# Combine rows and weights in one partition-first table; lists give its row and the token

## Chip, cores and metric

The kernel runs on one core of one Trainium2 chip. The metric is the device time of one execution in microseconds (us), the median of several runs. Engines: TensorE (PE; PEld is its weight load), VectorE (DVE), ScalarE (ACT), GpSimd (POOL) and SyncE (SP), which here only issues DMAs; a queue (SPq, ACTq, POOLq) is the sequencer that issues for its engine.

## What is computed

Three layers in a row, all in float32, on 4 x 768 = 3072 tokens of 512 numbers (8 heads of 64):

```python
# 1. retention, per head h, over t
state = gamma[h] * state + outer(k[t], v[t]);  y[t] = scale * q[t] @ state
# 2. soft mixture: 8 experts with 4 slots each
logits = x @ phi                              # [3072, 32]
slot_input = softmax(logits, axis=0).T @ x    # [32, 512]
slot_out[e] = relu(slot_input[e] @ w1[e]) @ w2[e]
x2 = softmax(logits, axis=1) @ slot_out       # rank 32: combine rows c @ slot_out
# 3. top-2 mixture of 8 experts on x2
noisy = x2 @ w_gate + log1p(exp(x2 @ w_noise)) * noise
top2, top2_w = two largest, softmax over the two
out[mask] += top2_w * (relu(x2[mask] @ v1[e]) @ v2[e])   # for each expert e
```

The weights of layer 3 are called v1 (512 x 1024) and v2 (1024 x 512) in the kernel.

## The kernel before

**Stages.** Retention runs over 24 chunks of 128 tokens (NCH = 24) until about 150 us. The soft mixture's slot experts follow; their weights W2 are loaded in eight DMAs of 2 MB, the last of them in two halves, and the stage accumulates in the PSUM tile `po` (L602). Within a chunk partition j holds token 2 * (j % 64) + j // 64.

**Low rank.** Since x2 is c @ slot_out with 32 columns in c, layer 3 never forms x2: for each expert, G[e] = slot_out @ v1[e] (32 x 1024) is made once (`g_dot`, split into two parts by `g_split`, copied to the four partition groups of the tile `gs` by 16 DMAs of `g_copy` on SyncE, L741, or by matmuls for expert 0, `g_rep`), and the hidden layer of a token is relu(c[token] @ G[e]).

**The table.** `ctab` in DRAM holds for each token 32 combine numbers and 8 routing weights, and a row N of zeros for unused list places. `combine()` (L561) makes the combine rows `cs` and writes them with two GpSimd DMAs (L577), one for each half of the partitions; `combine_t()` transposes them with six matmuls (L584) for the router's logits. The routing weights `wsl` are written later by two ScalarE DMAs (L692).

**Routing (193 to 225 us).** Logits (L633), noise and the two choices on VectorE (L642 to L663), ranks in the expert's list by matmuls (L669 to L674), rounding to a block `blk` and a place in the block `rr`. Between them stand `fill` matmuls on ones (L144), which compute nothing that is used; F1 to F4, FA and FT are their numbers. The weights go through ScalarE, GpSimd and VectorE (L682 to L690; L685 is a reciprocal).

**Lists.** `lists(e)` (L750) makes for experts 0 and 1 the list of tokens: a mask `bm` on VectorE, two products of it on GpSimd (`bt`, L757 and L758: with the chunk's base and with the token in the chunk), three one-hot tiles `oh` on VectorE, 24 matmuls into `pli`, and two VectorE instructions that add the two sums (L768, L770). `lists_all()` does this for experts 2 to 7 jointly, in steps between the blocks of experts 0 and 1: each step's tiles are first touched by a tiny ScalarE copy of a block's output (`mark`), so that they can't run before it. Its products with the choices, `sb` on GpSimd (L804), had no such mark.

**Experts (from 225 us).** For each expert, 6 blocks of 128 list places and one of 64: `fetch` gathers the table's rows by an indirect DMA on GpSimd (L851), `turn` splits and transposes them (L863 to L873), `hidden` multiplies with G and makes the ReLU in two parts (L904, L907 on ScalarE, L909 on VectorE), `main` multiplies with v2 in two parts (`split_hi` on ScalarE, L879; `split_lo` on VectorE, L885; matmuls L937 to L943), scales the output (`yo`, L946) and adds it to `out` by an indirect DMA (L918). Blocks run in the order 0, 1, 2, 3, 6, 4, 5 for expert 0. `load_paced` loads the next v2 in four DMAs of 512 KB, each behind a tiny ScalarE copy of a block's output (L957, DMA L958); v1 two experts further the same way. V1[2] is loaded in three quarters at L698 and a fourth at L995, behind a GpSimd copy (L994) of the first gathered row.

**Order.** A scheduler puts the instructions of each engine and queue in order: it takes what is ready by its own estimate of time, the earlier in the program first. `after(ins)` keeps what the block traces on the same engine behind `ins`. `HOOK[e, b, kf]` runs a function while block b of expert e is traced, at its kf-th slice.

## Time and profile before

| | us |
|---|---|
| median of 3 runs | 589.7 (586.41 to 592.46) |
| the profiled execution | 592.0 |
| its span, first to last instruction | 590.2 |
| TensorE busy in the span | 554.7 (94%) |
| VectorE, ScalarE, GpSimd busy | 255.3, 243.7, 222.5 |
| mean granted clock of TensorE | 0.964 of full |

Times in the profile are counted from the first instruction. A row of the timeline has its start, its duration, the engine, the line of the kernel, the operation, the tile written and the tiles read, shapes, how many instructions are merged in it, and in brackets how long the engine was idle before it and whose end let it go.

### The profile page before, as it was taken

How to read it: one execution, taken by the hardware profiler on the slowest of the kernel's cores; microseconds unless marked ns; L12 is line 12 of the kernel's file. 1: busy time of each engine (PE TensorE's matmuls, PEld its weight loads, DVE VectorE, ACT ScalarE, POOL GpSimd, SP SyncE). 2: the span in 40 equal slices, each digit the busy share in tenths (PEclk: the TensorE clock that was granted, in tenths of full speed). 3: DMA queues.
4: the chain of work that ended last, by engine and by line, in shares of the span. 5: the costliest groups of instructions: out<-in, count | busy, mean ns of one | idle time of the engine just before them, and what ended most of it. 6: DMA issues, size and time to landing. Idle time of an engine off the chain costs nothing. (4 is left out here: it accounts for less than half of the span.)

```text
span 590.2 us, 10723 instructions
## 1 busy us (share of the span) xinstructions
PE 554.7 (94%) x4196; PEld 421.8 (71%) x4196; DVE 255.3 (43%) x529; ACT 243.7 (41%) x543; POOL 222.5 (38%) x214
## 2 busy tenths in 40 slices
PE   7999999999899878979999999999999999999990
PEld 4787888787443436858787787787787787788880
DVE  3566777764202366456625235235235234334200
ACT  2555656553101235245246246246345335335210
POOL 3524534330103055642455444344344436332231
PEclk7899999999699789989999999999999999999997
DMA  9999999998799942465446646656656644553232
GB/s 218 286 270 306 299 328 281 308 405 364 291 404 389 367 124 67 102 179 151 108 98 182 125 132 186 124 151 168 137 140 170 143 112 65 132 105 46 37 43 31
DMA packets 79485, 111.76 MB, mean 189 GB/s; under 512 B 10066, under 2 KB 51602, under 8 KB 78530
## 3 DMA queue, kind: packets, MB, share of 16 engines
q1 hardware_dynamic: 65808, 95.96, 49.3%
q0 software_dynamic: 9696, 14.37, 16.7%
q10 hardware_dynamic: 3922, 0.66, 0.6%
q8 instruction: 35, 0.57, 0.4%
q14 instruction: 24, 0.20, 0.1%
HBM read 87.92 MB, written 20.41 MB: 184 GB/s over the span
## 5 line engine op out<-in xcount | busy, mean ns | idle before, releaser
L937 PE MATMUL pyc<-wh,hhl 128*128 128x512 f32 x384 | 154.6, 403 | 0.2 <-ACT hhl L907 0.2
L938 PE MATMUL pyc<-wl,hhl 128*128 128x512 f32 x384 | 152.1, 396 | 0.0
L939 PE MATMUL pyc<-wh,hhl 128*128 128x512 f32 x384 | 151.5, 395 | 0.0
L918 POOL DMA_INDIRECT out_dram<-yo,lsa x42 | 66.1, 1575 | 136.1 <-ACT w L957 31.6
L909 DVE SCALAR_TENSOR_TENSOR hhl<-phc,hhl 128x512 fp32r<-128x512 f32 (+1 forms) x128 | 66.9, 551 | 84.9 <-ACT hhl L907 84.5
L939 PEld LDWEIGHTS pyc<-wh,hhl 128*128 128x128 f32 x384 | 72.6, 189 | 16.6
L937 PEld LDWEIGHTS pyc<-wh,hhl 128*128 128x128 f32 x384 | 72.1, 188 | 16.1 <-ACT hhl L907 0.4
L946 ACT ACTIVATE yo<-pyc,cg 128x512 f32<-128x512 f32 x48 | 33.0, 688 | 121.0 <-PE pyc L939 108.1
L938 PEld LDWEIGHTS pyc<-wl,hhl 128*128 128x128 f32 x384 | 72.4, 189 | 14.6
L907 ACT ACTIVATE hhl<-phc 128x512 fp32r<-128x512 f32 (+1 forms) x128 | 59.5, 513 | 8.0 <-PE phc L904 6.6
L885 DVE TENSOR_TENSOR wl<-w,wh 128x1024 fp32r<-128x1024 f32 x32 | 39.1, 1225 | 49.6 <-ACT wh L879 49.6
L851 POOL DMA_INDIRECT cg<-ctab,lsa x42 | 43.8, 1042 | 15.2 <-issue 14.9
L879 ACT CAST wh<-w 128x1024 fp32r<-128x1024 f32 x32 | 33.4, 1047 | 32.3 <-DMA w<-in_moe_w_dram 24.7
L298 DVE TENSOR_TENSOR am<-pa,cta 128x512 f32<-128x512 f32 x48 | 33.1, 692 | 28.6 <-PE py L322 15.3
L918 POOL DMA_INDIRECT out_dram<-yo,ls x14 | 25.0, 1787 | 47.4 <-ACT w L957 16.2
L256 POOL TENSOR_TENSOR comp<-raws,cta 64x512 f32<-64x512 f32 x24 | 24.9, 1039 | 40.7 <-PE py L322 16.5
L276 DVE TENSOR_TENSOR qT<-pt,cta 64x512 f32<-64x512 f32 x48 | 33.0, 688 | 16.6 <-PE pt L271 16.2
L256 POOL TENSOR_TENSOR vl<-raws,cta 64x512 f32<-64x512 f32 x24 | 24.9, 1038 | 33.5 <-PE py L322 22.6
L904 PE MATMUL phc<-cts,gs 128*128 128x256 f32 (+1 forms) x192 | 36.5, 299 | 0.5 <-ACT cts L873 0.5
L904 PEld LDWEIGHTS phc<-cts,gs 128*128 128x128 f32 x192 | 29.8, 191 | 7.3 <-issue 2.5
L294 PE MATMUL pa<-qT,kT 64*128 64x128 f32 x384 | 31.7, 296 | 0.7 <-DVE qT L276 0.7
L294 PEld LDWEIGHTS pa<-qT,kT 64*128 64x128 f32 x384 | 27.0, 198 | 5.2 <-issue 3.7
(195 smaller groups left out, 701.6 us busy)
## 6 DMA issues: line engine op xcount, KB each, us to landing
w<-in_moe_w_dram SPq DMA_DIRECT2D x80, 512.0 KB, 5.1
w<-in_moe_w_dram SPq DMA_DIRECT2D x11, 2048.0 KB, 10.5
comp<-in_q_dram SPq DMA_DIRECT2D x12, 512.0 KB, 6.7
out_dram<-zt SPq DMA_DIRECT2D x6, 1024.0 KB, 9.8
raws<-in_k_dram SPq DMA_DIRECT2D x11, 512.0 KB, 5.6
raws<-in_v_dram SPq DMA_DIRECT2D x11, 512.0 KB, 7.8
gs<-gr SPq DMA_DIRECT2D x112, 32.0 KB, 2.3
w<-in_moe_w_dram SPq DMA_DIRECT2D x2, 1024.0 KB, 21.1
```

The lines of the kernel that those rows point to most:

```text
L256: pool_ins[0] = nc.gpsimd.tensor_tensor(VL[j][rs], RAW[u][1][gs, :, r, :], gv[gs, r, t, :, None].to_broadcast([64, H, D]), op=OP.mult)
L294: mm = nc.tensor.matmul(pa[s][:, hp, :], KT[j][r, hp, :], QT[t][r, hp, g, :], start=True, stop=True)
L851: nc.gpsimd.indirect_dma_start(out=cg[:rows(b), i, :], out_offset=None, in_=ctab, in_offset=index(e, b, rows(b)))
L879: ins = nc.scalar.copy(wh, V2[e][:, 1024 * i:1024 * i + 1024])
L885: nc.vector.tensor_tensor(wl, V2[e][:, 1024 * i:1024 * i + 1024], WH[e][i], op=OP.subtract)
L904: nc.tensor.matmul(ph[:, w * i:w * i + w], GS[e][:, kf + i], CT[e, g][:, :w], start=True, stop=True)
L907: relu.append(nc.scalar.activation(h[:, :, :w], pv, AF.Relu))
L909: last = nc.vector.scalar_tensor_tensor(h[:, :, w + t0:w + t0 + 2 * P], pv[:, :, :2 * P], 0.0, h[:, :, :2 * P], op0=OP.max, op1=OP.subtract)
L918: nc.gpsimd.indirect_dma_start(out=out, out_offset=index(e, b, n), in_=y, in_offset=None, bounds_check=N - 1, oob_is_err=False, compute_op ...
L937: nc.tensor.matmul(py, hhl[:, kf, ts], wh, start=(kf == 0), stop=False)
L938: nc.tensor.matmul(py, hhl[:, kf, ts], wl, start=False, stop=False)
L939: nc.tensor.matmul(py, hhl[:, kf, tl], wh, start=False, stop=(kf == KF - 1))
```

## The change

- `ctab` has N rows in the order partition first: row = 24 * partition + chunk. The zero row and its DMA are gone.
- Combine rows and weights lie in one tile `row` (128 partitions x 24 chunks x 40 numbers); `cs` and `wsl` are views of it. One ScalarE DMA writes it when the weights are there, in place of two GpSimd DMAs and two ScalarE DMAs.
- `combine_t` has 24 matmuls against the identity, with 32 columns of weights each, in place of 6 transposes, since four chunks are no longer neighbours.
- Lists: the second factor is the partition (`row`) in place of the token in the chunk (`tok`). From the two sums `places` makes two tables, `lg` (row of the table, for gathers) in two instructions and `ls` (token, for adding to `out`) in three more behind it.
- Fills in the routing: 14 before g_dot(0) and 6 behind it, in place of 26 before it. The reciprocal of the weights stands behind the sum of the two choices.
- All four quarters of V1[2] are loaded behind the table's DMA; the copy L994 and the DMA L995 are gone.
- `sb` of the joint lists gets a mark. The copy of G for expert 2 to `gs` moves from slice 6 of block 0 to slice 5 of block 3 of expert 0; its split stays.
- The path for lists that overflow uses both tables (not shown; it isn't taken with these inputs).

```diff
--- before.py
+++ after.py
@@ -41,7 +41,7 @@
 ZJ = 16, 17, 18, 18, 18, 18
 HV = 7
 FB, FN = 7, 6
-F1, F2, F3, F4 = 2, 0, 0, 26
+F1, F2, F3, F4, F5 = 2, 0, 0, 14, 6
 FA, FT = 6, 3
 RL = 1
 XB = 5
@@ -77,7 +77,7 @@
     cols, parts32 = {}, cols
     cols["tri"] = (j[:, None] < j[None, :]) - BIG * np.eye(P)
     cols["base"] = np.broadcast_to(C * np.arange(NCH)[None] - N, (P, NCH))
-    cols["tok"] = tok[:, None]
+    cols["row"] = j[:, None]
     cols["iota"] = np.broadcast_to(np.arange(P)[None] - (P - 1) / 2, (P, P))
     cols["iotab"] = np.broadcast_to(P * np.arange(NB)[None], (P, NB))
     cols["rev8"] = np.broadcast_to(E - np.arange(E)[None], (P, E))
@@ -166,14 +166,8 @@
 
     phis = ab.tile([P, KD, NS], F32, name="phis")
     LT = ab.tile([P, NG, P], F32, name="LT")
-    ctab = tc.dram_tile([N + 1, NS + E], F32, name="ctab")
-
-    def row_view(r):
-        return ctab[:N].rearrange("(c i r) s -> r i c s", c=NCH, r=2)[r]
-
-    zrow = consts.tile([1, NS + E], F32, name="zrow")
-    nc.vector.memset(zrow, 0.0)
-    nc.scalar.dma_start(ctab[N:N + 1, :], zrow)
+    ctab = tc.dram_tile([N, NS + E], F32, name="ctab")
+
     acc = ab.tile([P, DM], F32, name="acc")
     MZ = ab.tile([P, 2 * NG], F32, name="MZ")
     W1, W2, V1, V2 = {}, {}, {}, {}
@@ -492,7 +486,8 @@
         sotT = late.tile([P, KD, NS], F32, name="sotT")
         rr = late.tile([P, NCH * E], F16, name="rr")
         blk = late.tile([P, NCH * E], F16, name="blk")
-        wsl = late.tile([P, NCH, E], F32, name="wsl")
+        row = late.tile([P, NCH, NS + E], F32, name="row")
+        wsl = row[:, :, NS:]
         cnt = late.tile([1, E], F32, name="cnt")
         tab = late.tile([P, P, 8], F16, name="tab")
         nc.gpsimd.tensor_copy(tab, iota[:, :, None].to_broadcast([P, P, 8]))
@@ -554,7 +549,7 @@
         for i in range(2):
             nc.gpsimd.memset(ht[i], 0.0)
         nc.vector.transpose(ht[2].rearrange("p j s -> p (j s)"), hs.rearrange("p j s -> p (j s)"))
-        cs = small.tile([P, NCH, NS], F32, name="cs")
+        cs = row[:, :, :NS]
         mx, sm = (small.tile([P, NCH], F32, name=n) for n in ("mx", "sm"))
         G3 = NG // 2
 
@@ -573,15 +568,15 @@
             nc.vector.tensor_scalar_add(sm, sm, 1e-9)
             nc.vector.reciprocal(sm, sm)
             nc.vector.tensor_tensor(cs, cs, sm[:, :, None].to_broadcast(cb), op=OP.mult)
-            for r in range(2):
-                nc.gpsimd.dma_start(row_view(r)[:, :, :NS], cs[64 * r:64 * r + 64])
 
         def combine_t():
             for i in range(2):
                 pc = psB.tile([P, G3, P], F32, name="pcn", tag="pt")
                 for g in range(G3):
                     a = 4 * (G3 * i + g)
-                    nc.tensor.transpose(pc[:, g, :], cs[:, a:a + 4].rearrange("p i s -> p (i s)"), ident)
+                    for q in range(4):
+                        nc.tensor.matmul(pc[32 * q:32 * q + 32, g, :], cs[:, a + q], ident, start=True, stop=True,
+                                         skip_group_check=True)
                 nc.scalar.copy(cT[:, G3 * i:G3 * i + G3], pc)
 
         po = psB.tile([P, DM], F32, name="po", bufs=1)
@@ -636,7 +631,9 @@
         pgd = [psB.tile([P, QF], F32, name="pg0", bufs=1), psB.tile([P, QF], F32, name="pg1", tag="pst", bufs=1)]
         with after(mm):
             fill(psB, "pw", F4, 1)
-            g_dot(0, pgd[0])
+            mm = g_dot(0, pgd[0])
+        with after(mm):
+            fill(psB, "pw", F5, 1)
         lo = small.tile([P, NCH, E], F32, name="lo")
         sp = small.tile([P, NCH, E], F32, name="sp")
         nc.scalar.activation(sp, pr[:, :, E:], AF.Exp)
@@ -660,7 +657,7 @@
             sels.append(se)
             tops.append(m)
         selh = small.tile([P, NCH * E], F16, name="selh")
-        nc.vector.tensor_add(selh, sels[0].rearrange("p c e -> p (c e)"), sels[1].rearrange("p c e -> p (c e)"))
+        both = nc.vector.tensor_add(selh, sels[0].rearrange("p c e -> p (c e)"), sels[1].rearrange("p c e -> p (c e)"))
 
         tc_h = small.tile([P, 2, P], F16, name="tc_h")
         nc.gpsimd.memset(tc_h[96:], 1.0)
@@ -682,19 +679,19 @@
         nc.gpsimd.tensor_tensor(w[:, 0], tops[1], tops[0], op=OP.subtract)
         nc.scalar.activation(w[:, 0], w[:, 0], AF.Exp)
         nc.gpsimd.tensor_scalar(w[:, 1], w[:, 0], 1.0, 1e-9, op0=OP.add, op1=OP.add)
-        nc.vector.reciprocal(w[:, 1], w[:, 1])
+        with after(both):
+            nc.vector.reciprocal(w[:, 1], w[:, 1])
         nc.gpsimd.tensor_tensor(w[:, 2], w[:, 0], w[:, 1], op=OP.mult)
         wse = small.tile([P, NCH, E], F32, name="wse")
         for i, t in enumerate((wsl, wse)):
             nc.gpsimd.tensor_tensor(t, sels[i], w[:, 1 + i, :, None].to_broadcast([P, NCH, E]), op=OP.mult)
         nc.gpsimd.tensor_tensor(wsl, wsl, wse, op=OP.add)
-        for r in range(2):
-            put = nc.scalar.dma_start(row_view(r)[:, :, NS:], wsl[64 * r:64 * r + 64])
+        put = nc.scalar.dma_start(ctab.rearrange("(p c) s -> p c s", p=P), row)
         V1[2] = ringp.tile([P, 4096], F32, name="w", tag="w")
         v1p = v1[2].rearrange("(k p) n -> p k n", p=P)
         with after(put):
-            nc.scalar.copy(V1[2].rearrange("p (k n) -> p k n", k=KD)[0:1, :KD - 1, 0:1], wsl[0:1, :KD - 1, 0:1])
-        for i in range(KD - 1):
+            nc.scalar.copy(V1[2].rearrange("p (k n) -> p k n", k=KD)[0:1, :, 0:1], wsl[0:1, :KD, 0:1])
+        for i in range(KD):
             nc.sync.dma_start(V1[2][:, 1024 * i:1024 * i + 1024], v1p[:, i])
 
 
@@ -745,7 +742,19 @@
         g_dot(e, pg)
         g_copy(e, g_split(pg, 1), 0)
 
-    LS = {}
+    LS, LG = {}, {}
+
+    def places(pool, pl, shape, sfx=""):
+
+        lt, la = (pool.tile(shape, F32, name=n + sfx, bufs=1) for n in ("lt", "la"))
+        lg, ls = (pool.tile(shape, I32, name=n + sfx, bufs=1 if sfx else None) for n in ("lg", "ls"))
+        nc.vector.tensor_scalar(lt, pl[:, 0], 1.0 / C, float(NCH), op0=OP.mult, op1=OP.add)
+        ins = nc.vector.scalar_tensor_tensor(lg, pl[:, 1], float(NCH), lt, op0=OP.mult, op1=OP.add)
+        with after(ins):
+            nc.vector.tensor_scalar(la, pl[:, 1], 64.0, -127.0, op0=OP.is_ge, op1=OP.mult)
+            nc.vector.scalar_tensor_tensor(la, pl[:, 1], 2.0, la, op0=OP.mult, op1=OP.add)
+            nc.vector.scalar_tensor_tensor(ls, lt, float(C), la, op0=OP.mult, op1=OP.add)
+        return ins, lg, ls
 
     def lists(e, pool, ps, nb):
         rv = rr.rearrange("p (e c) -> p e c", e=E)
@@ -755,7 +764,7 @@
                                 col16("iotab")[:, None, :nb].to_broadcast([P, NCH, nb]), op=OP.is_equal)
         bt = pool.tile([P, NCH, 2, nb], F16, name="bt", bufs=1)
         nc.gpsimd.tensor_tensor(bt[:, :, 0, :], bm, col16("base")[:, :, None].to_broadcast([P, NCH, nb]), op=OP.mult)
-        nc.gpsimd.tensor_tensor(bt[:, :, 1, :], bm, col16("tok")[:, :, None].to_broadcast([P, NCH, nb]), op=OP.mult)
+        nc.gpsimd.tensor_tensor(bt[:, :, 1, :], bm, col16("row")[:, :, None].to_broadcast([P, NCH, nb]), op=OP.mult)
         oh = pool.tile([P, NCH // 8, P, 8], F16, name="oh", bufs=1)
         for c in range(NCH // 8):
             nc.vector.tensor_tensor(oh[:, c], tab, rv[:, e, None, 8 * c:8 * c + 8].to_broadcast([P, P, 8]),
@@ -764,12 +773,9 @@
         for c in range(NCH):
             mm = nc.tensor.matmul(pl.rearrange("p a b -> p (a b)"), oh[:, c // 8, :, c % 8], bt[:, c].rearrange("p a b -> p (a b)"),
                              start=(c == 0), stop=(c == NCH - 1))
-        lt = pool.tile([P, nb], F32, name="lt", bufs=1)
-        nc.vector.tensor_scalar_add(lt, pl[:, 0, :], float(N))
-        ls = pool.tile([P, nb], I32, name="ls")
-        last = nc.vector.tensor_tensor(ls, lt, pl[:, 1, :], op=OP.add)
-        LS[e] = ls
-        return mm, last
+        last = places(pool, pl, [P, nb])
+        LG[e], LS[e] = last[1:]
+        return mm, last[0]
 
     def lists_all():
 
@@ -800,7 +806,8 @@
             y = yield
             bt = cc.tile([P, NCH, 2, E, LB], F16, name="bta", bufs=1)
             sb = cc.tile([P, 2, NCH, E], F16, name="sb", bufs=1)
-            for a, name in enumerate(("base", "tok")):
+            for a, name in enumerate(("base", "row")):
+                mark(sb[0:1, a, 0, 0:1], y)
                 nc.gpsimd.tensor_tensor(sb[:, a], sels[i], col16(name)[:, :, None].to_broadcast([P, NCH, E]),
                                         op=OP.mult)
                 mark(bt[0:1, 0, a, 0, 0:1], y)
@@ -814,18 +821,15 @@
                                  start=(i == 0 and c == 0), stop=(i == 1 and c == NCH - 1))
             if i == 0:
                 y = yield
-        lt = cc.tile([P, E, LB], F32, name="lta", bufs=1)
-        nc.vector.tensor_scalar_add(lt, pl[:, 0], float(N))
-        ls = cc.tile([P, E, LB], I32, name="lsa", bufs=1)
-        nc.vector.tensor_tensor(ls, lt, pl[:, 1], op=OP.add)
+        lg, ls = places(cc, pl, [P, E, LB], "a")[1:]
         for e in range(2, E):
-            LS[e] = ls[:, e]
+            LG[e], LS[e] = lg[:, e], ls[:, e]
         for g in range(G):
             fetch(2, g)
         yield
 
-    def index(e, b, n=P):
-        return bass.IndirectOffsetOnAxis(ap=LS[e][:n, b:b + 1], axis=0)
+    def index(lists, e, b, n=P):
+        return bass.IndirectOffsetOnAxis(ap=lists[e][:n, b:b + 1], axis=0)
 
     G = SB // 2
 
@@ -849,7 +853,7 @@
             nc.gpsimd.memset(cg[TL:, 2, :], 0.0)
         for i, b in enumerate(bs):
             nc.gpsimd.indirect_dma_start(out=cg[:rows(b), i, :], out_offset=None, in_=ctab,
-                                         in_offset=index(e, b, rows(b)))
+                                         in_offset=index(LG, e, b, rows(b)))
             WT[e, b] = cg[:rows(b), i, NS + e:NS + e + 1]
 
     def turn(e, g, hold=()):
@@ -915,7 +919,7 @@
         return last, relu
 
     def add_rows(e, b, y, n=P):
-        nc.gpsimd.indirect_dma_start(out=out, out_offset=index(e, b, n), in_=y, in_offset=None,
+        nc.gpsimd.indirect_dma_start(out=out, out_offset=index(LS, e, b, n), in_=y, in_offset=None,
                                      bounds_check=N - 1, oob_is_err=False, compute_op=OP.add)
 
     def main(e, g):
@@ -985,14 +989,11 @@
         g_dot(2, pg2, range(KD - 1))
         fill(psC, "pyc", FA)
         fetch(0, 0)
-        cg0 = CG[0, 0]
         ga = turn(0, 0)
         fill(psC, "pyc", FT)
         with after(*ga):
             for g in range(1, G):
                 fetch(0, g)
-            nc.gpsimd.tensor_copy(V1[2][0:1, 3072:3073], cg0[0:1, 0, 0:1])
-            nc.sync.dma_start(V1[2][:, 3072:], v1p[:, 3])
         for i in range(4):
             if i > 1:
                 split_hi(0, i)
@@ -1011,9 +1012,11 @@
             HOOK[0, 4, 4] = HOOK[1, 1, 2] = next, gen
     def g_rest():
         g_dot(2, pg2, [KD - 1])
-        g_copy(2, g_split(pg2, 1), 0)
-
+        gr2.append(g_split(pg2, 1))
+
+    gr2 = []
     HOOK[0, 0, 6] = g_rest,
+    HOOK[0, 3, 5] = (lambda: g_copy(2, gr2[0], 0)),
     for e in range(E):
         pre = {g: [] for g in range(G)}
         if e + 1 < E:
...
```

## Rows read from the trace of the kernel before

**Rows 1.** Windows: length, busy of PE, PEld, DVE, ACT, POOL, PEclk, DMA share, GB/s

```profile
258.00:261.00 3.00, 3.00 (x11) 2.54 (x10) 0.00 (x0) 1.39 (x4) 0.00 (x0) 0.50 0.60 102
261.00:574.00 313.00, 313.00 (x1592) 249.14 (x1591) 120.12 (x247) 133.81 (x306) 129.65 (x102) 1.00 0.54 123
```

**Rows 2.** The timeline, TensorE's weight load before the last W2 half

```profile
192.59 0.16 PEld L602 LDWEIGHTS po<-w,ht 128*32 128x32 f32 x8 [0.80 <-DMA w<-in_moe_w_dram]
```

**Rows 3.** DMA queues, 183 to 194 us: packets, MB, share of 16 engines

```profile
q0 software_dynamic: 128, 0.39, 11.5%
```

**Rows 4.** The timeline, TensorE: small matmuls in retention, and combine_t

```profile
64.66 1.08 PE L356 MATMUL pl<-xT,phis 128*32 128x128 f32 x32
...
183.53 0.85 PE L584 MATMUL pcn<-ct,cs 128*128 128x128 f32 x6
```

**Rows 5.** The timeline of the routing, 199 to 209 us

```profile
199.29 7.72 PE L144 MATMUL pw<-ones 128*128 128x512 f16 x26
...
203.13 3.38 PEld L144 LDWEIGHTS <-ones 128*128 128x128 f16 x16 [0.28 <-issue]
...
206.23 0.30 DVE L685 RECIPROCAL w<-w 128x24 f32<-128x24 f32 x1 [0.47 <-POOL w L684]
...
207.17 0.46 DVE L663 TENSOR_TENSOR selh<-sel,sel 128x192 f16<-128x192 f16 x1
...
208.70 1.54 ACTq L692 DMA_DIRECT2D ctab<-wsl  x2
...
208.80 0.31 PE L669 MATMUL pt<-ones,selh 128*96 128x128 f16 x2
```

**Rows 6.** The timeline of expert 0's list and first gather, 211 to 223 us

```profile
211.81 0.33 DVE L754 TENSOR_TENSOR bm<-blk,ct 128x168 f16<-128x168 f16 x1
...
212.03 1.98 POOL L804 TENSOR_TENSOR sb<-sel,ct 128x192 f16<-128x192 f16 x2 [3.36 <-PE pg L185]
...
214.86 0.47 POOL L758 TENSOR_TENSOR bt<-bm,ct 128x168 f16<-128x168 f16 x1
...
215.37 1.57 PE L765 MATMUL pli<-bt,oh 128*128 128x14 f16 x24 [3.45 <-POOL bt L758]
...
217.63 1.91 POOL L851 DMA_INDIRECT cg<-ctab,ls  x1 [2.31 <-DVE ls L770]
...
222.55 0.24 ACT L863 CAST cts<-cg 128x64 fp32r<-128x64 f32 x1
```

**Rows 7.** The timeline of expert 1's list, mask and second product

```profile
228.16 0.33 DVE L754 TENSOR_TENSOR bm<-blk,ct 128x168 f16<-128x168 f16 x1
...
229.38 0.91 POOL L758 TENSOR_TENSOR bt<-bm,ct 128x168 f16<-128x168 f16 x1
```

**Rows 8.** The page's DMA issues: count, KB each, median us from issue to landing

```profile
ctab<-cs POOLq DMA_DIRECT2D x2, 192.0 KB, 8.0
...
cg<-ctab,ls POOLq DMA_INDIRECT x14, 2.4
```

**Rows 9.** The timeline of SyncE's queue, 215 to 262 us

```profile
215.68 2.53 SPq L741 DMA_DIRECT2D gs<-gr  x3
227.79 0.34 SPq L995 DMA_DIRECT2D w<-in_moe_w_dram  x1
...
228.18 18.97 SPq L741 DMA_DIRECT2D gs<-gr  x29
247.25 14.96 SPq L958 DMA_DIRECT2D w<-in_moe_w_dram  x5
```

**Rows 10.** The timeline of the hole: block 0's mark, V2[1]'s cast, expert 1's turn

```profile
237.81 0.19 ACT L957 COPY w<-yo 1x1 f32<-1x1 f32 x1
...
252.43 1.05 ACT L879 CAST wh<-w 128x1024 fp32r<-128x1024 f32 x1 [4.06 <-DMA w<-in_moe_w_dram]
...
257.75 0.67 PE L870 MATMUL ptc<-identr,st 128*128 128x128 f32 x3 [3.72 <-DVE st L865]
```

**Rows 11.** The timeline, GpSimd's scatter at the joint lists' first products

```profile
261.60 2.81 POOL L918 DMA_INDIRECT out_dram<-yo,ls  x1 [4.62 <-ACT w L957]
```

4 lines of the change are left out of this document (3 added, 1 removed).

## The prediction

> **What bounds the kernel now.** I read the engines by stretch first. From 261 to 574 us TensorE is busy for 313.00 of 313.00 us, and before that it has only short holes [rows 1]. So whatever makes the expert stage start earlier, or closes a hole in its beginning, is carried to the end, and nothing else can be. The change touches two such places. One is the routing stage, a chain in which one engine waits for the other: logits, the two choices, ranks, the lists of expert 0, the first gather, the first expert matmul. The other is a hole at 254 us. The timeline gives the links of both, the queue of SyncE and the DMA page the rest.
>
> **Before the chain: the table's combine half.** The combine weights go out in two DMAs while the slot experts' W2 loads run. The last W2 half makes TensorE wait 0.80 us at 192.59 [rows 2]. In that stretch of 11 us the table's packets take 11.5% of the DMA engines, 1.27 us of all sixteen [rows 3]. The change takes them out of it; the load lands by up to 1.27 earlier, and the 0.80 can be had and no more. Against it stands combine_t: 24 small matmuls for 6 transposes. The nearest row with the new shape, 128x32 weights and 128 columns in the four column strips, has 32 in 1.08 us, so 24 take 0.81; the 6 transposes take 0.85 [rows 4]. I take 0.7 us; bounds 0 and 0.8.
> If instead the 24 ran one after another at a transpose's 0.85 / 6 = 0.14 us, they would take 3.4 us, 2.55 more, and instead of a gain of 0.7 there would be a loss of 2.55 - 0.80 = 1.75 [rows 2, 4]; the row with their own shape says that four strips run at once. A rule speaks for that dearer price: the Trainium skill (TensorE: Matmul & The Clock Gate, Terms) holds that transpose mode is 4 times faster for FP32, so that plain matmuls in place of the 0.85 us would take 3.4 too, by an estimate from that page; no run here has yet shown this stage without transposes.
>
> **Fills and the order on VectorE.** 26 filling matmuls run from 199.29, the first 9 in 3.84 us (0.43 each) and from 203.13 at 0.21 each; then, at 199.29 + 7.72 = 207.0, come the 32 matmuls of g_dot(0), and only behind them, at 208.80, the first matmul of the ranks, 1.8 us later, though its input was done at 207.17 + 0.46 = 207.63 [rows 5]. After the change: 14 fills end at 203.13 + 5 x 0.21 = 204.2, g_dot(0) at 206.0, 6 more fills at 207.3, and with 0.1 for the issue the ranks begin at 207.4. The input comes earlier too: the reciprocal, which now waits for the sum of choices, had held VectorE 0.47 us idle and then 0.30 of its own; taking 0.65 of these 0.77 the sum is done at 207.0. TensorE is the later one, at 207.4: gain 1.4 us. Bounds: 0.3, if all 14 fills ran at 0.43, and 1.8, if the sum alone decided.
> The reciprocal moves the other way, by 207.0 - 206.23 = 0.8 us, and the routing weights on GpSimd with it, and the table's DMA behind them: it was issued at 208.70 [rows 5], now at 209.5, less the 0.7 from above 208.8.
>
> **Joint lists' product held.** GpSimd is free when expert 0's block mask (bm, 211.81) is coming, but two products for the joint lists, needed 50 us later, take it for 1.98 us from 212.03. The list's own products end at 214.86 + 0.47 = 215.33, 3.52 us after bm began, and the list's matmuls wait 3.45 us for them [rows 6]. Expert 1's list has no such intruder: there it is 229.38 + 0.91 - 228.16 = 2.13 us [rows 7]. The mark now holds the intruder until a later block: gain 3.52 - 2.13 = 1.4 us. Bounds: 0 (GpSimd is taken by something else), 1.98.
>
> **What is late next.** These three make 3.5 us, and the first gather would be issued at 217.63 - 3.5 = 214.1 [rows 6]. It needs the whole table. One DMA with 3,840 B in a row for each partition is in no row: gathers land in a median of 2.4 us, the old combine writes took 8.0 in a saturated stretch [rows 8]. From 208.8 that is 211.2 or 216.8. It runs on nearly empty engines, so I stay near the first, and it is hidden; at the far end the gather loses 2.7. The two list tables cost one instruction more in number but not in length before the gather; the three VectorE instructions behind it, at most 0.30 each by the reciprocal [rows 5], stand before the splits, which have until the cast at 222.55 [rows 6]. The fourth quarter of V1[2] now loads with the other three, ahead of the gather on the same engines; I allow nothing for it. The removed zero row and its DMA were off every chain: no gain.
>
> **The hole at 254 us.** SyncE sends expert 1's and expert 2's copies of G. After the first three (215.68 + 2.53 = 218.2) the V1[2] quarter that waits for a gather holds the queue until 227.79; then 29 copies take 18.97 us, 0.65 each [rows 9]. The first quarter of V2[1] could go from the mark on block 0's output at 237.81, but goes at 247.25 [rows 9, 10]. Its cast on ScalarE waits 4.06 us for it, until 252.43; behind it in ScalarE's queue stand ReLUs and the turn of expert 1, and TensorE stands still for 3.72 us at 257.75 [rows 10]. Then the granted clock is 0.50, the lower of its levels, for 3 us [rows 1]: the same work at the upper level takes half, and I count 1.4 us. After the change the waiting quarter is gone from the queue and expert 2's 16 copies come later in the program. Expert 1's 13 open copies need 13 x 0.65 = 8.5 us from 218.2; shifted by 3.5 they are through by 223. The V2[1] quarter goes at 237.81 - 3.5 = 234.3, lands 5.2 us later (as 247.25 to 252.43), and the cast, wanted at 252.43 - 4.06 - 3.5 = 244.9, finds it there. Gain 3.7 + 1.4 = 5.1 us; bounds 0 and 5.1. The 16 copies, when they come, cost 10.4 us of the queue behind block 3; only the later quarters of V2[1] and V1[3] stand behind them, and I allow nothing for those.
>
> **What it costs.** The joint products now run at two block ends on GpSimd behind a scatter, which took 2.81 us there [rows 11], and VectorE's product waits in order for them, with the hidden layer's splits behind it. Without the cover of the early run that is up to 2.81 + 1.98 / 2 = 3.8 us at each of two places; TensorE has queued work for part of it, and the split already in hand can go ahead. I charge 0.5 us; bounds 0 and 7.6.
>
> **Sum.** 0.7 + 1.4 + 1.4 + 5.1 - 0.5 = 8.1 us. The profiled execution took 592.0 us (span 590.2), so it would take 583.9. The median of the three runs before is 589.7, 2.3 lower than the profiled one; the same difference gives 581.6 us.
>
> **Rivals.**
> Forecast, both places gain: 581.6; own range 579.0 (the charge is zero and the other small holes go too) to 584.5 (fills and hold give half). Chance 0.54.
> Copies still first: the order of a queue is made by a scheduler that takes what is ready; if expert 2's copies are ready before the mark on block 0, all 16 (10.4 us) go before V2[1] as now. For it: the joint products ran 50 us early in just this way [rows 6]. Against it: the V2[1] loads now stand earlier in the program. Only 3.0 us are gained: 586.7. Chance 0.21.
> The gather comes no earlier: the table lands late, or V1[2]'s 2 MB hold the gather. For it: the write moves 0.8 us nearer while the gather comes 3.5 nearer. Against it: 2.9 us between the two at 2.4 us landing. It takes 2.8 of the gain: 584.4. Chance 0.12.
> Transposes one after another: with the 3.4 us above, 8.1 - 0.7 - 1.75 = 5.65 are gained, 584.0. Chance 0.02.
> It does not do what it says, both gains fail: 589. Chance 0.05.
> Slower: at the two joint products VectorE waits the full 3.8 us for GpSimd, the splits starve TensorE, and each hole brings the lower clock (1.4 as above): 2 x 5.2 = 10.4 against 8.6 gained, 591.5; it turns the sign from 4.3 us each. With the hole at 254 left it is 596.6. For it: VectorE works in order. Against it: the first four splits can go before the product. Chance 0.06.
>
> **Numbers.** Predicted 581.6 us. From 578.5 to 588.5 the forecast, the copies' rival, the late gather and the transposes are in, about 0.8. A measurement of this kernel can tell about 1% from no change, so faster means below 583.8 and slower above 595.6. Faster: 0.85 of the forecast's chance (0.46), under half of the late gather's and the transposes' (0.06): 0.52. Slower: the part of the last rival in which the hole stays too, and what I do not see: 0.04. The same: 0.44.
>
> **What would show it.** Right: no TensorE wait for W2 before the last half; the ranks' first matmul about 2.1 us earlier; expert 0's list products within 2.2 us of its mask; the first gather issued near 214.1 in place of 217.63; the first V2[1] load within 2 us of block 0's mark; no hole and no lower clock in block 3. Wrong: the 16 copies in front of that load; a first gather waiting for the table's DMA or landing over 3 us; VectorE idle before the joint products with TensorE waiting behind.

## The result: slower by 0.6%, and the profile after

The changed kernel takes 592.79 us (median of 20 runs, 587.39 to 595.86), the kernel before beside it 589.37 (20 runs, 583.98 to 595.71): ratio 1.0059, 95% interval 1.0036 to 1.0083. The forecast was 581.6 us, a gain; it is a loss of 3.4, within the 1% that the forecast called no change, but outside its range. The profiled execution took 595.86 us, the longest of the 20; its span is 594.1. Ratios, here and below, leave out single executions more than 1.5% above the fastest of their kernel: two of x12_rest_held's and one of b2_zero_row_third's.

The windows first, with the columns of [rows 1]: the three bad stretches, the place of the old hole, and the long stretch of [rows 1].

```profile
222.00:231.00 9.00, 7.39 (x27) 5.66 (x28) 6.54 (x12) 3.64 (x11) 4.63 (x5) 0.62 0.24 58
254.00:258.00 4.00, 4.00 (x21) 3.24 (x20) 0.55 (x3) 1.24 (x3) 1.51 (x1) 1.00 0.79 176
262.00:269.00 7.00, 4.33 (x15) 3.29 (x14) 5.99 (x15) 2.23 (x7) 0.09 (x1) 0.70 0.61 169
292.00:300.00 8.00, 5.54 (x36) 4.74 (x35) 5.76 (x10) 1.24 (x2) 3.35 (x3) 0.79 0.36 90
261.00:574.00 313.00, 307.87 (x1552) 244.90 (x1551) 120.53 (x248) 131.77 (x297) 124.71 (x102) 0.98 0.53 121
```

The hole at 254 us is closed, as forecast, and the rival "copies still first" is out: SyncE issues V2[1]'s first quarter at 238.95, 0.2 us behind block 0's mark at 238.73. But from 261 to 574 us TensorE, busy for 313.00 of 313.00 us at clock 1.00 before [rows 1], is now busy for 307.87 at 0.98, and two new holes make that: 2.67 us idle in 262 to 269, 2.46 in 292 to 300, each with the lower clock behind it.

The waits from 255 to 300 us and the timeline name the cause. In order: VectorE's waits for GpSimd's joint products in total; GpSimd's first pair; VectorE's product of it; the two TensorE instructions that stood.

```profile
DVE bta L814 <- POOL sb L811: 7.9, 2, 5.2
...
260.34 1.56 POOL L811 TENSOR_TENSOR sb<-sel,ct 128x192 f16<-128x192 f16 x2
...
261.47 3.32 DVE L814 TENSOR_TENSOR bta<-bma,sb 128x1344 f16<-128x1344 f16 x2 [2.68 <-POOL sb L811]
...
265.40 0.60 PE L908 MATMUL phc<-cts,gs 128*128 128x320 f32 x1 [2.67 <-DVE hhl L916]
...
294.71 1.57 PE L819 MATMUL pli<-bta,oh 128*128 128x112 f16 x19 [2.46 <-DVE bta L814]
```

GpSimd gets to the held products only behind its scatter, VectorE waits for them in order, 2.68 and 5.18 us, and then makes its two products of 3.32 us together. TensorE lacks what comes of that: at the first hole the split `hhl`, which stands behind VectorE's products, at the second the products themselves, for which the list's matmuls wait in TensorE's order.

The routing, where [rows 5] and [rows 6] stood: ranks, list, first gather, its cast, and TensorE up to the first expert matmul.

```profile
206.96 0.31 PE L666 MATMUL pt<-ones,selh 128*96 128x128 f16 x2 [1.11 <-DVE selh L660]
212.15 1.59 PE L774 MATMUL pli<-bt,oh 128*128 128x14 f16 x24 [2.08 <-POOL bt L767]
214.99 1.35 POOL L855 DMA_INDIRECT cg<-ctab,lg  x1 [2.89 <-DVE la L754]
221.59 0.25 ACT L867 CAST cts<-cg 128x64 fp32r<-128x64 f32 x1 [2.38 <-issue]
222.58 0.63 PE L179 MATMUL pg<-w,sotT 128*32 128x256 f32 x6
226.16 0.80 PE L908 MATMUL phc<-cts,gs 128*128 128x256 f32 x2 [0.49 <-DVE gr L717]
226.76 0.63 PE L941 MATMUL pyc<-wh,hhl 128*128 128x512 f32 x1
```

The first gather is issued 2.6 us earlier than in [rows 6], but 6.6 us pass until its cast instead of 4.92, and the last matmuls of expert 2's product of G (L179, six records), which need V1[2]'s fourth quarter, now run ahead of the first expert matmul. That matmul comes at 226.76; before it came at 225.25.

The start of the program I had not looked at. ScalarE's issue of the constant table, its first copy of K and TensorE's first transpose, before:

```profile
1.74 0.36 ACTq L420 DMA_DIRECT2D cta<-in_const_a_dram  x1
...
4.99 1.25 ACT L255 COPY comp<-raws 64x512 f32<-64x512 f32 x2 [1.10 <-DMA raws<-in_k_dram]
...
6.29 0.66 PE L283 MATMUL pt<-ct,comp 128*128 128x128 f32 x4 [0.86 <-ACT comp L255]
```

and after:

```profile
1.14 0.45 ACTq L414 DMA_DIRECT2D cta<-in_const_a_dram  x1
...
6.50 1.25 ACT L249 COPY comp<-raws 64x512 f32<-64x512 f32 x2 [2.94 <-DMA raws<-in_k_dram]
...
7.80 0.66 PE L277 MATMUL pt<-ct,comp 128*128 128x128 f32 x4 [2.31 <-ACT comp L249]
```

The zero row's DMA, which the change removes, had held the 356 KB table back by 0.6 us. Now the table goes out earlier, the first tile of K lands 1.5 us later, and TensorE starts 1.5 later.

### The profile page after: what moved, and what is told of

It reads as the page before. It is cut to its first block, busy times and chain, and to the rows that moved or that the text cites. A ratio compares the mean times of both kernels' runs of the same rounds, so it can differ in the third digit from the quotient of the medians.

```text
span 594.1 us, 10799 instructions
## 1 busy us (share of the span) xinstructions
PE 556.0 (94%) x4232; PEld 425.2 (72%) x4232; DVE 256.3 (43%) x537; ACT 244.1 (41%) x547; POOL 216.9 (37%) x211
## 5 line engine op out<-in xcount | busy, mean ns | idle before, releaser
L941 PE MATMUL pyc<-wh,hhl 128*128 128x512 f32 x384 | 156.0, 406 | 0.0
L943 PE MATMUL pyc<-wh,hhl 128*128 128x512 f32 x384 | 153.6, 400 | 0.0
L943 PEld LDWEIGHTS pyc<-wh,hhl 128*128 128x128 f32 x384 | 73.2, 191 | 17.2
L941 PEld LDWEIGHTS pyc<-wh,hhl 128*128 128x128 f32 x384 | 73.3, 191 | 15.3
L855 POOL DMA_INDIRECT cg<-ctab,lga x42 | 41.2, 981 | 24.6 <-issue 22.2
L922 POOL DMA_INDIRECT out_dram<-yo,ls x14 | 23.8, 1703 | 47.8 <-ACT hhl L911 17.8
L908 PEld LDWEIGHTS phc<-cts,gs 128*128 128x128 f32 x192 | 30.3, 196 | 12.2 <-issue 6.3
```

What stands on the lines that cost most here:

```text
L855: nc.gpsimd.indirect_dma_start(out=cg[:rows(b), i, :], out_offset=None, in_=ctab, in_offset=index(LG, e, b, rows(b)))
L908: nc.tensor.matmul(ph[:, w * i:w * i + w], GS[e][:, kf + i], CT[e, g][:, :w], start=True, stop=True)
L922: nc.gpsimd.indirect_dma_start(out=out, out_offset=index(LS, e, b, n), in_=y, in_offset=None, bounds_check=N - 1, oob_is_err=False, comput ...
L941: nc.tensor.matmul(py, hhl[:, kf, ts], wh, start=(kf == 0), stop=False)
L943: nc.tensor.matmul(py, hhl[:, kf, tl], wh, start=False, stop=(kf == KF - 1))
```

## The experiments

The chip grants TensorE the lower clock (0.50) in spells whose number, place and length differ from trace to trace, and executions of one kernel differ by several us, in part with it (x6_first_dma: 581.24 us at a mean clock of 0.986, 585.87 at 0.967). So verdicts rest on the ratio to the kernel before, run beside on the same chip, and causes on landmarks that I read in all 17 traces (us; `pst` is TensorE's first transpose of the slot outputs, 194.41 in the kernel before). "Stage" is from the first expert matmul to the issue of the last scatter, "end" from there to the end of the span.

| kernel | median | ratio [95%] | first transpose | gather - pst | first expert matmul - pst | stage | end |
|---|---|---|---|---|---|---|---|
| before | 589.4 | 1 | 6.29 | 23.22 | 30.84 | 352.8 | 12.2 |
| after | 592.79 | 1.0059 [1.0036, 1.0083] | 7.80 | 19.24 | 31.01 | 357.0 | 10.3 |
| x1_sb_early | 589.89 | 1.0003 [0.9978, 1.0028] | 7.94 | 19.23 | 31.45 | 351.1 | 10.4 |
| x14_sb_free | 590.29 | 1.0018 [0.9991, 1.0045] | 7.81 | 19.93 | 32.90 | 350.3 | 10.7 |
| x2_quarter_back | 593.98 | 1.0067 [1.0042, 1.0093] | 7.76 | 19.62 | 28.85 | 355.4 | 10.5 |
| x3_both | 586.64 | 0.9945 [0.9917, 0.9973] | 7.75 | 20.94 | 30.15 | 348.5 | 10.5 |
| x12_rest_held | 588.60 | 0.9972 [0.9940, 1.0004] | 7.61 | 19.22 | 32.03 | 353.0 | 10.6 |
| x11_after_first_dma | 591.46 | 1.0045 [1.0019, 1.0072] | 5.79 | 19.61 | 32.46 | 355.4 | 10.4 |
| x6_first_dma | 584.20 | 0.9883 [0.9841, 0.9925] | 5.91 | 19.61 | 28.97 | 353.6 | 10.5 |
| x7_phi_first | 584.19 | 0.9892 [0.9847, 0.9938] | 6.37 | 19.22 | 26.48 | 351.2 | 10.4 |
| x8_copy_back | 586.71 | 0.9959 [0.9929, 0.9989] | 7.79 | 19.60 | 28.69 | 350.4 | 10.4 |
| x9_best | 585.86 | 0.9927 [0.9902, 0.9952] | 6.28 | 19.23 | 27.72 | 352.6 | 10.3 |
| x10_table_later | 588.14 | 0.9968 [0.9936, 1.0000] | 6.03 | 19.24 | 27.03 | 357.7 | 10.5 |
| x13_small_rows | 585.54 (one run) | - | 6.26 | 19.24 | 27.84 | 350.2 | 10.4 |
| b1_copy_later | 590.07 | 1.0018 [0.9990, 1.0045] | 6.39 | 21.19 | 30.82 | 350.5 | 12.2 |
| b2_zero_row_third | 591.08 | 1.0025 [0.9995, 1.0055] | 7.59 | 21.27 | 29.01 | 353.1 | 12.0 |
| b3_fills | 589.71 | 1.0001 [0.9974, 1.0027] | 6.46 | 20.35 | 29.99 | 350.6 | 12.4 |

### Joint lists' products: held later, held earlier, not held

x1_sb_early moves the products to an earlier block:

```diff
+            # in the step that makes rk, two blocks earlier
+            sb = cc.tile([P, 2, NCH, E], F16, name="sb", bufs=1)
+            for a, name in enumerate(("base", "row")):
+                mark(sb[0:1, a, 0, 0:1], y)
+                nc.gpsimd.tensor_tensor(sb[:, a], sels[i], ...)
```

> The changed kernel, with one thing different: the joint lists' products of choices on GpSimd (sb) are held by the mark of the step two blocks earlier (block 1 and block 4 of expert 0) and not by that of the step that uses them (block 3 of expert 0, block 0 of expert 1). Theory A (VectorE waits in order for sb, the hidden layer's splits stand behind it): both holes of TensorE, 2.7 us near 265 and 2.5 us near 294, go, and with them the lower granted clock behind each, about 1.2 us: 592.8 - 7.5 = 585.3 us. Theory B (the loss is made before the first expert matmul, by a late first gather and by expert 2's split in front of the hidden layer): nothing moves, 592 to 593. Theory C (the table's new order makes all gathers slower): nothing moves either.

x14_sb_free takes the hold alone away (`- mark(sb[0:1, a, 0, 0:1], y)`).

> The changed kernel without the hold of the joint lists' products: GpSimd does the first two of them ahead of list 0's, as before the change, all else as changed. Theory J (the hold lets them start too late for the joint lists, which then stop VectorE and TensorE twice, 2.67 and 2.46 idle in the changed kernel's trace with 3.4 lost to the lower clock behind them): both waits go, the first gather is issued 1.0 to 2.0 later than at 19.24 from the end of the slot experts, and the time is 592.8 - 5.1 + 1.0 to 2.0, some 589 to 590, no worse than x1_sb_early's 589.9 by more than 1. Forecast's view (the hold gains 1.4 and costs 0.5): 592.8 + 0.9 = 593.7.

By the ratios they win back 3.3 and 2.4 us of the 3.5 that the changed kernel loses by its own: x14's median is about what theory J gave, x1's is 4.6 above what was expected. In both traces the two holes are gone; the window of x1 that answers to the changed kernel's third:

```profile
262.00:269.00 7.00, 7.00 (x51) 5.83 (x51) 4.57 (x18) 2.83 (x8) 0.56 (x2) 1.00 0.60 171
```

So the hold, where the change put it, takes the kernel from level to slower. x14 also prices what the hold gives; GpSimd's pair, the list's matmuls and the first gather in its trace:

```profile
210.33 1.42 POOL L810 TENSOR_TENSOR sb<-sel,ct 128x192 f16<-128x192 f16 x2 [1.13 <-PE pg L179]
...
213.56 1.58 PE L774 MATMUL pli<-bt,oh 128*128 128x14 f16 x24 [3.34 <-POOL bt L767]
...
215.83 1.90 POOL L854 DMA_INDIRECT cg<-ctab,lg  x1 [2.32 <-DVE la L754]
```

The list's matmuls wait 3.34 us in place of 2.08, but the gather, counted from `pst`, is only 0.7 later (19.93 against 19.24); theory J had 1.0 to 2.0.

### V1[2]'s fourth quarter

x2_quarter_back puts the quarter's load back behind the first gather, x3_both does that and x1's move:

```diff
-        for i in range(KD):
+        for i in range(KD - 1):
             nc.sync.dma_start(V1[2][:, 1024 * i:1024 * i + 1024], v1p[:, i])
...
+            nc.gpsimd.tensor_copy(V1[2][0:1, 3072:3073], cg0[0:1, 0, 0:1])
+            nc.sync.dma_start(V1[2][:, 3072:], v1p[:, 3])
```

> The changed kernel, with the fourth quarter of V1[2] again behind the first gather, as in the kernel before; so the copies of G wait in SyncE's queue again until the gather has landed, and expert 2's last products and split can't come before the hidden layer. Theory B: the second gather lands about 2.4 us after its issue (4.9 in the changed kernel), no split of expert 2 before the first expert matmul, which comes 3 to 5 us earlier counted from the end of the slot experts; the holes at the joint products stay: 588 to 590 us. Theory A: the holes are what counts, 592. Theory C: the gather still lands late, about 4.9 us, and 592.

> The changed kernel with both: sb held two blocks earlier, and the fourth quarter of V1[2] behind the first gather. Theories A and B together: the sum of the two gains, 592.8 - 7.5 - 3.5 = about 581.8 us. If A alone is right 585, if B alone is right 589; if the hole at 254 us comes back with the held quarter, 5 us more.

With the holes at the joint lists in place the quarter gives nothing that can be measured (x2 against after); with them mended it gives 3.3 us (x3 against x1, on one chip). x3 came to 586.6, where the two gains together would have made 581.8. x2's traced execution took 589.70, one of its two shortest, so its row in the table is not that of its median. The landmark shows it in either case: in the five traces with the quarter early the first expert matmul comes 31.0 to 32.9 us behind `pst`, in the eight with it late 26.5 to 30.2, without overlap; the means are 32.0 and 28.2. The gather and the cast that reads it, x1 and then x3:

```profile
214.95 1.34 POOL L856 DMA_INDIRECT cg<-ctab,lg  x1 [2.88 <-DVE la L754]
...
222.07 0.24 ACT L868 CAST cts<-cg 128x64 fp32r<-128x64 f32 x1 [2.87 <-DMA cg<-ctab,lg]
```

```profile
217.31 1.33 POOL L856 DMA_INDIRECT cg<-ctab,lg  x1 [2.87 <-DVE la L754]
...
222.15 0.28 ACT L868 CAST cts<-cg 128x64 fp32r<-128x64 f32 x1
```

7.12 us with the quarter early, 4.84 with it late, 4.92 before [rows 6]; over the traces 5.4 to 7.1 early, 4.5 to 4.8 late, 4.9 to 5.4 without the change. So the new table's layout costs the gather nothing; the delay goes with the early quarter. Whether the early product of G costs as well was the question of x12_rest_held (x1 with that product held behind the sixth expert matmul):

```diff
-        g_dot(2, pg2, [KD - 1])
+        with after(*MM):
+            g_dot(2, pg2, [KD - 1])
```

> The kernel x1_sb_early with expert 2's last quarter of the product of G held behind the first expert's sixth matmul, as it stood before the change; the quarter itself still loads early. If the product in the wrong place is what costs: the gap of 1.46 ahead of the first expert matmul goes, as do the 0.57 of the product, that matmul starts at about 29.4 from the end of the slot experts instead of 31.45, and the time is 589.9 - 2.0 = 587.9. If it is the late gather (issue to the cast that reads it 7.12 against 4.84 in x3_both): the matmul starts at 30.9 or later and the time is 589.4 to 589.9.

Neither came out as put. The product was held, yet the first expert matmul stood at 32.03, because ScalarE's cast behind the transposes began late:

```profile
224.61 0.37 ACT L878 CAST cts<-ptc 128x256 fp32r<-128x256 f32 x1 [4.48 <-remote]
225.03 1.65 PE L909 MATMUL phc<-cts,gs 128*128 128x256 f32 x6 [4.43 <-ACT cts L878]
```

By the profile, which models the ends of matmuls, the transposes had been done since 220.6. `<-remote` marks a wait that was ended by a semaphore whose sender the view does not name. In the trace's records it is the semaphore that TensorE's matmuls raise, raised at 224.58; in 16 of the 17 traces this cast begins 0.03 us behind such a signal. So ScalarE was waiting, and TensorE's signal came 4.0 us behind the modelled end. It came 2.5 us behind it in x11, 2.1 in x14, 1.7 in b1 and at most 1.3 in the others where it is recorded; why, no run shows. By the ratios x12 is 1.8 us faster than x1, with intervals that overlap. How the 3.8 us between the two means divide between the late gather, the product and such late signals stays open.

### The start: one DMA of 160 bytes

b2_zero_row_third is the kernel before with the zero row's DMA behind the table and phi; x11_after_first_dma, and x6_first_dma on top of x3, put it back in front in the changed kernel (into a row that nothing reads); x7_phi_first is x3 with phi's 64 KB ahead of the table; x10_table_later does both of these on x9_best (below).

```diff
+    ztab = tc.dram_tile([1, NS + E], F32, name="ztab")   # x6, x10, x11
+    nc.scalar.dma_start(ztab, zrow)
...
+        nc.scalar.dma_start(phis, ...)                   # x7, x9, x10: moved up
         nc.scalar.dma_start(cta, csta)
```

> The kernel before with nothing changed but the place of the zero row's DMA in ScalarE's queue: behind the constant table and the phi load instead of ahead of them. Theory S: the constant table is issued at about 1.15 as in the changed kernel, the first TensorE transpose starts at 7.8 instead of 6.3, and the time is 589.4 + 1.0 = 590.4. Rival (something else of the change makes the late start): 6.3 and 589.4. The end stays at 12.2 from the last scatter's issue.

> The kernel x3_both with the zero row's DMA put back in its old place in ScalarE's queue, right behind the first constant table (into a row of DRAM that nothing reads). In the four traces with the change the first TensorE transpose of K starts at 7.75 to 7.94 us, in the two without it at 6.29 and 6.39; the DMA of the 356 KB constant table is issued at 1.14 in the first and at 1.74 in the second, because the row's DMA of 0.52 no longer stands ahead of it. Theory S (the earlier constant table takes the DMA engines from the first K tile): first transpose at 6.3, and what is left of the 1.5 at the end of the slot experts is about 1.0 (194.79 against 195.75 at one clock), so the median is x3's 586.6 less 1.0 = 585.6. Rival: the start is not set by this DMA: 7.8 and 586.6. The end of the program: from the issue of the last scatter to the end of the span is 12.2 without the change and 10.4 with it; if the row's DMA makes that, 1.8 come back and the median is 587.4.

> The kernel x3_both with the 64 KB phi load issued ahead of the 356 KB constant table on ScalarE's queue, no DMA added: the constant table is issued at about 1.6 instead of 1.14, the phi load at 1.14 instead of 1.62. Theory S: the first K tile lands earlier again, first transpose between 6.3 and 7.0, and the median is 586.6 less 0.7 to 1.0, 585.7. Rival (the sum of bytes ahead of K counts, and phi's 64 KB are now early too, or the start is set elsewhere): 7.8 and 586.6. The end of the program stays at 10.4 from the last scatter, since no row of zeros is written.

> The changed kernel with the zero row's DMA put back alone. Theory S: first transpose at 5.9 to 6.3 instead of 7.80 and 592.8 less 1.0 to 2.5 (x6 against x8 on one chip 2.5, the traces at the end of the slot experts 1.0): 590.3 to 591.8. If the other two losses hide what the start gives, 592.8. By x6 against x3 (ratio 0.9883 against 0.9945) it would be 3.6, 589.2.

> The kernel x9_best with the zero row's DMA of 0.52 issued as well, ahead of phi and the constant table, so that the constant table is issued at about 2.1 us (x6 1.70, x7 1.62, the changed kernel 1.14). Theory S, taken further: the first transpose starts at 5.9 or earlier (x6 5.91, x7 6.37, the changed kernel 7.80) and the time is x9's less 0 to 0.5. Rival: the table itself is late now and the products that need it wait: the first transpose is early, but the first product of K with Q comes later than x6's 9.74, and the time is x9's plus up to 0.5.

The first transpose follows the issue of the table in every trace: 7.6 to 7.9 us with the issue at 1.14 to 1.18, 5.8 to 6.5 with it at 1.62 or later. b2, with one line moved, and x6:

```profile
1.18 0.44 ACTq L419 DMA_DIRECT2D cta<-in_const_a_dram  x1
...
7.59 0.69 PE L282 MATMUL pt<-ct,comp 128*128 128x128 f32 x2 [2.70 <-ACT comp L254]
```

```profile
1.70 0.36 ACTq L418 DMA_DIRECT2D cta<-in_const_a_dram  x1
...
5.91 0.66 PE L281 MATMUL pt<-ct,comp 128*128 128x128 f32 x4 [0.41 <-ACT comp L253]
```

That the place of this DMA sets the start is shown. How the earlier table slows K is not: in the first 3.5 us SyncE's queue, which carries K, moved 0.23 MB before, 0.24 in x6 and 0.21 in x7, but 0.13 after and 0.14 in b2, while ScalarE's queue, which carries the table, moved 0.14 to 0.15 in all five, so the table's bytes alone do not account for it. What of the 1.5 us reaches the end is measured less well: 3.6 and 3.1 (the ratios of x6 and x7 against x3's), 2.5 (the medians of x6 and x7 against x8 in one batch), 1.9 (the ratios of x9 and x8), 0.8 (those of x11 and after), 1.5 for b2, whose interval reaches to zero. All have one sign, and `pst` comes at 193.1 us on the mean of the nine traces with the early start, at 194.5 on that of the other eight; I take 1 to 2 us, an estimate. Going further than 1.7 (x10) brings the start no earlier, and its median is 2.3 above x9's, with intervals that overlap, instead of at most 0.5 off. Its first product of K with Q comes at 10.23, later than x6's 9.74, as the rival had it, but ahead of x9's 10.73, so the 2.3 are not made there. In its trace the time lies in the stage, where TensorE stands for 2.17, 1.64 and 1.59 us at 297, 321 and 366 us.

### The hole at 254 us

b1_copy_later is the kernel before with only the move of expert 2's copies; x8_copy_back is x3 with this move undone, x9_best is x7 with it undone.

```diff
-        g_copy(2, g_split(pg2, 1), 0)        # in g_rest
+        gr2.append(g_split(pg2, 1))
+    HOOK[0, 3, 5] = (lambda: g_copy(2, gr2[0], 0)),
```

> The kernel before, with one thing changed: the copies of expert 2's G come at slice 5 of block 3. It prices the hole at 254 us by itself. If the first quarter of V2[1] no longer stands behind these 16 copies, the hole of 3.7 us and the lower clock behind it (1.4) go: 589.4 - 5.1 = 284 less than 585, that is 584.3 us. If the hole only wanders (the turn of expert 1 waits for something else), 588 to 589.

(The number meant is the 584.3 at its end.)

> The kernel x3_both with the one move undone that was to take the hole at 254 us away: expert 2's copies of G are issued in one go where they stood before the change. Forecast's term H: the hole comes back, 3.7 of idle TensorE with some 1.4 at the lower clock behind it, 586.6 + 5.1 = 591.7. Rival (the run of the kernel before with only this move, 590.07, gained nothing, so the hole's work only changes its place): 586.6 with the hole back, and other gaps gone. TensorE's idle time of 0.4 us and more behind 210 us is 3.04 in x3; H expects 6.7.

> The kernel x7_phi_first (joint lists' products two blocks earlier, the fourth quarter of V1[2] behind the first gather, phi loaded ahead of the constant table) with expert 2's copies of G issued where they stood before the change. If the move of the copies is worth nothing once the gather is early (x8_copy_back 586.71 against x3_both 586.64), the median is that of x7, 584.2. If it is worth the forecast's 5.1, it is 589.3. In x7's trace the moved copies leave a gap of 2.57 at 244.25 us with 1.7 lost to the lower clock behind it, in x8 a gap of 1.50 at 252.13 and no lower clock: by these two traces 584.2 less 1.1 to 2.8, 581.4 to 583.1.

Where the copies are moved the hole is never there. Where they are not it is 3.72 us (before), 3.90 (b2), 1.65 (x9) and 1.50 (x8), and it is absent in b3, x10 and x13. Its 5.1 us do not follow it: b1 gains nothing (590.07, interval -0.6 to +2.7 us), x8 is level with x3, and x9's median is 1.7 above x7's, from another chip and with intervals that overlap. TensorE's wait at this place in b2, which has neither move nor earlier gather, and in x8:

```profile
252.81 0.51 PE L870 MATMUL ptc<-identr,st 128*128 128x128 f32 x3 [3.90 <-DVE st L865]
```

```profile
252.13 0.52 PE L875 MATMUL ptc<-identr,st 128*128 128x128 f32 x3 [1.50 <-DVE st L870]
```

With the gather early and nothing moved, 1.50 are left of the 3.90. In b3_fills, which does not touch the copies either, ScalarE's cast of V2[1] waits only 0.47 us for its load (4.26 in b2, 1.90 in x8), and the hole is not there at all. That what TensorE loses earlier, to a wait or to the lower clock, comes off the hole is my reading of this; no run singles it out. And in all eleven traces with the copies moved, a wait for VectorE stands at 244 to 251 us in its stead, 0.7 to 2.6 long (b1 1.13, x3 1.13, x6 1.33, x7 2.57). Why b1, which moves nothing but the copies, gains nothing in the median stays open: the stage of its trace is 2.3 us shorter than that of the one before.

### Fills and reciprocal

b3_fills does these two in the kernel before:

```diff
-F1, F2, F3, F4 = 2, 0, 0, 26
+F1, F2, F3, F4, F5 = 2, 0, 0, 14, 6
```

> The kernel before with two parts of the change in the routing alone: 14 fills ahead of expert 0's products and 6 behind them instead of 26 ahead, and the reciprocal of the weights behind the sum of the selections. The forecast put 1.4 on the two: 589.4 - 1.4 = 588.0. Rival: the 1.4 was read from an execution in which the fills ran at the lower clock (26 in 7.72 us; 5.78 in the trace of b2_zero_row_third, where TensorE then waits 0.71 for VectorE anyhow), so only the 0.7 of the reciprocal is there, and less where the gather is not the end of the wait: 588.7 to 589.4.

Level with the kernel before, interval -1.5 to +1.6 us. The ranks begin 11.21 us behind `pst` and the gather is issued at 20.35. To see what the two gave, the trace must be one whose routing ran at the full clock, as b3's did up to its list; in b2's the 26 fills and the ranks read:

```profile
194.80 5.78 PE L144 MATMUL pw<-ones 128*128 128x512 f16 x26
...
203.15 0.31 PE L669 MATMUL pt<-ones,selh 128*96 128x128 f16 x2 [0.71 <-DVE selh L663]
```

The fills take 5.78 us in place of 7.72 [rows 5], and TensorE waits for VectorE already; the ranks begin at 12.00, the gather goes at 21.27. The gain is 0.8 at the ranks and 0.9 at the gather, and since TensorE waited there for VectorE (in the changed kernel too, 1.11 us), by this trace it is the reciprocal's, not the fills'.

### The end of the program

x13_small_rows is x9 with the weights also written out in 32-byte rows, as before the change:

```diff
+        for r in range(2):
+            nc.scalar.dma_start(wv[r], wsl[64 * r:64 * r + 64])
```

> The kernel x9_best with the weights also written out in 3,072 rows of 32 bytes by two more DMAs on ScalarE's queue, as before the change, into a table that nothing reads. The trace is read for one thing: from the issue of the last scatter to the end of the span it is 12.0 to 12.5 in the four traces that write these rows (3,922 packets on that queue) and 10.3 to 10.5 in the nine that do not (960 packets). If the packets make it, it is 12.2 here; if not, 10.4. The time itself is some 1 to 3 above x9's, since the two DMAs' issues stand ahead of V1[2]'s load.

ScalarE's queue has its packets back, and the end is 583.7 - 573.28 = 10.42 all the same:

```profile
q10 hardware_dynamic: 4064, 1.15, 0.9%
...
573.28 1.55 POOL L927 DMA_INDIRECT out_dram<-yo,lsa  x1 [4.00 <-DMA out_dram<-yo,lsa]
```

It is not the packets, and not the zero row's DMA either: x6 and x11, which write that row, end at 10.5 and 10.4. All 13 traces with the change end 10.3 to 10.7 us behind the last scatter's issue, the four without it 12.0 to 12.4. The trace's records say where the difference lies: GpSimd's last two long instructions, an INC_SWDGE_SEM and a DRAIN, take 1.41 and 5.06 us in the four, 1.04 and 3.50 in the 13. The two GpSimd DMAs of the combine rows are a part of the change that no run put back; whether they make the difference is not shown.

## Why the prediction was wrong

**The joint lists' products were mis-sized; this decides the sign.** The step that failed, and that turns the gain into a loss, is the charge of 0.5 us (bounds 0 and 7.6) for the held products. It rested on "TensorE has queued work for part of it, and the split already in hand can go ahead" and, among the rivals, on "the first four splits can go before the product". At the first place the work in hand did not suffice, 2.67 us of hole. At the second it was not the splits: the list's matmuls need the product itself and stand in TensorE's order, 2.46 us. The lower clock follows both. Over the traces the stage is 356.0 us with the hold in its late place (three), 351.9 without (ten), 351.7 before (four): 4.1 us; in the time 2.4 to 3.3 by the ratios of x14 and x1, and 7.3 by the medians of x2 and x3, where the quarter is mended. With the products moved to an earlier block the kernel is level with the one before (1.0003). This is the mechanism of the rival that I gave 0.06. That its 591.5 came nearest is luck: its sum has 10.4 us of loss, where 4.1 were measured, against 8.6 of gain, which did not come.

**"I allow nothing for it", the quarter:** with it the first expert matmul is 3.8 us later by the means above, against a gain of 2.0 that the early gather brings where the quarter stays (30.2 in the four traces without the change, 28.2). The rival "V1[2]'s 2 MB hold the gather" named the right place and was too cheap at 2.8. The losses do not simply add: with the hold in its late place the quarter gave nothing (x2), with the hold moved 3.3 us.

**"Off every chain: no gain", the zero row:** true of the row itself. What stood behind it on its own queue I did not look at: the table's load got 0.6 us earlier and K landed 1.5 later, by estimate 1 to 2 us lost.

**The hole, 5.1 us: right in the trace, wrong in the sum.** It was counted as if independent of the 3.5 us of the routing and of the clock. The same earlier gather that was booked as a gain also shortens the hole (1.50 in x8 against 3.90 in b2); that is not the whole of it, since b1 gains nothing without an earlier gather. Without the late hold the stage is 351.3 us in the six traces of the changed kernel with the move, 352.7 in the four without it, 351.7 in the kernel before and its three variants (350.5 in b1, which has the move), and single traces spread from 348.5 to 357.7: no gain of 5.1.

**Fills 1.4 and hold 1.4: half right.** Gather 0.9 and 0.7 earlier in traces at the same clock. The 1.4 of the fills was read from an execution whose fills ran at the lower clock; I saw the 0.43 and the 0.21 and did not ask whether the next execution would have them. At the full clock VectorE, not TensorE, is the later one at the ranks. The hold did what it was to do at the list's products, which end 2.13 us behind the mask, but only 0.7 of its 1.4 reached the gather. With all of the change the gather comes 2.0 earlier behind `pst` (19.24 against 21.19 and 21.27), where the forecast had 2.8, its 3.5 less the 0.7 ahead of `pst`; of the 4.0 between the two profiled executions the other half is the lower clock of [rows 5].

**The combine half, 0.7: no gain that the traces show.** The 0.80 in [rows 2] stood on the weight load; TensorE's own row has no gap there. That wait is gone in all 13 traces with the change, as forecast, but TensorE had lost nothing by it before, and 0.36 in b1. And plain f32 matmuls leave two records each:

```profile
184.47 1.52 PE L578 MATMUL pcn<-ct,row 128*32 128x128 f32 x48
```

24 matmuls, 48 records; so "32 in 1.08" [rows 4] were 16, as were the "32 matmuls of g_dot(0)", and 24 cost 1.52, not 0.81. The four strips do overlap: in the trace's records four start within 0.05 us of each other, and such fours follow every 0.11 us, as single transposes do before. By the Trainium skill's rule (TensorE: Matmul & The Clock Gate, Terms), that transpose mode is 4 times faster for FP32, it would be 3.4, an estimate from the 0.85 of the transposes. The trace does not agree: 1.52 is 1.8 times.

**In sum.** Of the signs that the forecast named, the gather (214.99 for 214.1), the list's products and the closed hole came true; so did the last of the wrong ones, VectorE idle before the joint products with TensorE waiting behind. With the three losses undone (x6, x7) the ratio is 0.9883 and 0.9892, 6 to 7 us faster, with x9 0.9927, 4 us. They beat both kernels; the three do not differ beyond their intervals. So most of the forecast's 8.1 us was there to be had, in part from other places (2.0 before the first expert matmul, 1.8 at the end, not the hole). What failed on the side of the costs were two zeros, the quarter and the zero row, and the half microsecond; on the side of the gains the 5.1 of the hole, and of the other 3.5 all but 2.0.

## What to carry to other kernels

Go through every instruction that a change removes or releases and ask what stood behind it in its own queue, DMA issues at the start of the program too: a freed queue pulls transfers forward, and another transfer can land later for it. A hold that clears one path wants its new deadline worked out, with what its engine does there and who waits in order behind it. Two savings on one meeting point, here an early gather and a hole that waits for a load, are not added, and a duration from a stretch at the lower clock is not carried to the next execution.
